# A new written order for five engines, new release points for late loads, and wider declarations of independence, in a fused attention and gated-convolution kernel

## The chip, the cores and the metric

The kernel runs on one core of one Trainium2 chip. The metric is device time in microseconds (us) for one execution; smaller is better. The engines are called PE (matrix products), ACT (activations and copies), DVE (vector arithmetic), POOL (here mostly the issue of software DMAs) and SP (the issue of hardware DMAs and DMA transposes).

## What is computed

There are 4 batches, 8 heads, 768 positions and 64 features per head. The attention is block sparse: 24 blocks of 32 positions, of which a query block sees its neighbours, the first and the last block, and three sampled ones. Its result, 512 features per position, goes through a feed-forward part with a depthwise convolution as the gate.

```python
scores = scale * np.matmul(q, k.transpose(0, 1, 3, 2))
scores = np.where(mask, scores, -1000000000.0)
attn = np.exp(scores - np.max(scores, axis=-1, keepdims=True))
attn = attn / (np.sum(attn, axis=-1, keepdims=True) + 1e-09)
x = np.matmul(attn, v)                       # then heads side by side: 512 features
h = np.maximum(x @ w_in, 0.0)                # 1024 features
conv_out = sum(conv_w[j] * hp[:, j:j + S, :] for j in range(3))   # hp is h, padded by one position
out = (h * (1.0 / (1.0 + np.exp(-conv_out)))) @ w_out
```

## The kernel before

**Units and segments.** The masked scores are taken densely: the mask is 24 more rows of the score product. The work is cut into 144 units. A unit is one PSUM tile of 128 keys by 1024 query columns (`st`, two of them): two halves of score products (operation `s`, line 746), one exponential on ACT over all 1024 columns (`exp`, line 757), which writes one of eight buffers `pt`, and two halves of four times two products with V (`av`, line 779). Units are numbered in the order in which they are worked; 18 of them make a segment, half a batch, and the last half batch is cut into a segment of 12 units and one of 6, so that there are nine segments, n = 0 to 8.

**A segment after its units.** DVE takes reciprocals and normalises (`rcp`, `norm`), the token tile is transposed by a DMA on SP (`x_xb`), or for seven tiles by PE with a copy behind it (`x_tr`, `x_cp`). Then come, for each of 8 groups of 128 features, the first product (`f1`, line 895, into one of two PSUM tiles `mix`), a relu out of PSUM into the feature tile `hE` on ACT (line 915) or on DVE (line 917), and, for each pair of groups, the convolution on DVE (`mul` line 949, `add` line 959), a tanh on ACT (`tanh`, line 998) and the gate on DVE (`g1` line 1001, `g2` line 1006). The segment n = 8 has its convolution on PE (`conv`, line 970). The second product (`f2`, line 825, line 810 for the last block of 128 rows) goes into `mix` too, is copied out by ACT or DVE (`ev`, through the helper `dcopy` at lines 328 and 330) and stored by a DMA on SP (`out`). While the feed-forward part of one segment is worked, the units of the next go on.

**Loads.** K, Q and V of a pair of heads are loaded by POOL. The pairs P = 0 to 3 belong to batch 0, and so on. From batch 2 on, each of these loads stands behind a `pace`: a copy of one element of the buffer `pt` of a named unit, by which POOL waits until the exponential of that unit is done. Such a copy reads `pt`, so the exponential that writes the same buffer eight or more units later has to wait for it.

**What sets the order.** Every operation is entered in a list `gr.ops` with its engines and an assumed cost for each, a due time, dependences and buffers. A search outside the kernel found an order; its result stands in the string `ORDER`. Only this string decides what is issued: for each operation it names the engine, where there is a choice, and the buffer. `put_down` walks through it, and calls the function that issues the instructions.

```python
            o = ops[64 * CODE.index(line[x]) + CODE.index(line[x + 1])]
            engines = list(o.alts)
            e = engines[0]
            if len(engines) > 1:
                e = ENGINES[line[x]]
            for b in o.allocs:
                b.index = CODE.index(line[x])
            if o.fn is not None:
                o.fn(e)
```

Costs, due times, earliest times and dependences in the list are not looked at here. The framework below adds a semaphore wait wherever two instructions on different engines touch the same tile and one of them writes. It takes a tile's columns in strides coarsely, which is why `apart` declares some pairs of instructions on `hE` independent: those that touch other columns of it.

## Time and profile before

| | |
|---|---|
| time of three executions, median (lowest to highest) | 204.87 us (204.59 to 204.95) |
| span of the profiled execution, first to last instruction | 202.8 us |
| time of the profiled execution itself | not listed apart from its span; the median lies 2.07 us above the span |
| busy PE, ACT, DVE, POOL | 196.8, 189.7, 181.8, 57.5 us |
| granted TensorE clock, mean | 0.998 |

A busy time is the union of an engine's instructions, in which pipelined matmuls overlap. A group of instructions shows its busy time, the mean duration of one in nanoseconds (with the overlap counted in), and the idle time of its engine ahead of it with what ended it. The chain of waits is followed back from the last instruction: it names, for each stretch of time, the instruction that held up the end.

### The profile page before, as it was taken

What the parts mean: (1) busy time and instruction counts of PE and PEld (TensorE: products, weight loads), DVE (VectorE), ACT (ScalarE), POOL (GpSimd) and SP (SyncE); (2) the same over time, 40 slices, a digit from 0 to 9 for tenths busy, and PEclk for the clock granted to TensorE, in tenths of its full rate; (3) what the DMA queues carried; (4) which work ended last, traced back from release to release, by engine and by line L of the source; (5) the groups of instructions that cost most, each with busy time, mean ns of one, the idle gap of its engine ahead of it and who ended that gap; (6) DMA issues with size and microseconds to landing.
All of it is one profiled execution on the core that took longest, in us unless ns stands there. A gap on an engine that the chain in (4) does not pass through costs nothing.

```text
span 202.8 us, 6814 instructions
## 1 busy us (share of the span) xinstructions
PE 196.8 (97%) x2708; PEld 153.9 (76%) x2708; DVE 181.8 (90%) x572; ACT 189.7 (94%) x251; POOL 57.5 (28%) x112
## 2 busy tenths in 40 slices
PE   7899999999999999999999999999999999999993
PEld 7799977986788777877688877876678877876742
DVE  7999989999999979999899988999899968999950
ACT  6999999999999999999999998999999989998842
POOL 8870568630520354202534328400000000000000
PEclk9999999999999999999999999999999999999999
DMA  6999999999998399956869699994321202001515
GB/s 143 177 223 207 182 135 132 167 171 151 155 122 129 61 141 154 213 106 132 133 108 159 82 197 218 135 176 115 124 72 24 41 14 68 13 10 60 204 63 202
DMA packets 53655, 25.96 MB, mean 128 GB/s; under 512 B 39616, under 2 KB 50584, under 8 KB 53624
## 3 DMA queue, kind: packets, MB, share of 16 engines
q0 software_dynamic: 19984, 11.24, 43.7%
q1 hardware_dynamic: 33208, 13.87, 34.6%
q8 instruction: 21, 0.34, 0.7%
q10 hardware_dynamic: 432, 0.43, 0.6%
q14 instruction: 10, 0.08, 0.1%
HBM read 23.08 MB, written 6.29 MB: 145 GB/s over the span
## 4 chain that ended last, share of the span: by engine, by line
PE 78%; ACT 15%; issue 3%; DVE 2%; DMA 1%; ACTq 0%
PE st L746 25%; PE mix L895 18%; PE mix L825 17%; PE av L779 14%; ACT pt L757 11%; DMA o2s<-in_k_dram 1%; DVE e L330 1%; ACT m L998 1%; PE mix L810 1%; PE st L825 1%; PE av L970 1%; ACT nat L328 1%; PE mix L508 1%; ACT hE L915 0%; ACT o2s L328 0%
## 5 line engine op out<-in xcount | busy, mean ns | idle before, releaser
L757 ACT ACTIVATE pt<-st 128x1024 bf16<-128x1024 f32 x144 | 140.6, 1039 | 1.8 <-PE st L746 0.9
L779 PE MATMUL av<-vt,pt 128*128 128x65 bf16 x1152 | 59.9, 193 | 0.2 <-DVE vt L330 0.2
L779 PEld LDWEIGHTS <-pt 128*128 128x128 bf16 x1152 | 52.3, 97 | 9.9 <-issue 0.3
L895 PE MATMUL mix<-xT,winb 128*128 128x384 bf16 (+2 forms) x288 | 53.6, 308 | 0.1
L949 DVE TENSOR_SCALAR m<-hE,cw 128x382 bf16<-128x382 bf16 (+2 forms) x192 | 49.3, 316 | 0.5 <-ACT hE L915 0.2
L825 PE MATMUL mix<-woutb,gT 128*128 128x512 bf16 x176 | 47.1, 379 | 0.3 <-DVE gT L1006 0.3
L746 PE MATMUL st<-o 88*128 88x128 bf16 (+1 forms) x240 | 43.9, 229 | 0.4 <-ACT pt L757 0.3
L746 PE MATMUL st<-o,e 88*128 88x128 bf16 (+1 forms) x228 | 43.4, 233 | 0.0
L746 PE MATMUL st<-e,o 88*128 88x128 bf16 (+1 forms) x224 | 42.3, 234 | 0.2 <-ACT pt L757 0.2
L746 PE MATMUL st<-e 88*128 88x128 bf16 (+1 forms) x208 | 40.9, 239 | 0.1
L746 PEld LDWEIGHTS <-o 88*128 88x128 bf16 x464 | 34.7, 97 | 7.7 <-issue 0.8
L746 PEld LDWEIGHTS <-e 88*128 88x128 bf16 x436 | 33.0, 97 | 7.1 <-issue 0.4
L959 DVE TENSOR_TENSOR m<-m 128x764 bf16<-128x764 bf16 (+2 forms) x64 | 33.5, 532 | 0.4
L895 PEld LDWEIGHTS <-winb 128*128 128x128 bf16 x288 | 24.0, 97 | 8.0 <-issue 0.5
L998 ACT ACTIVATE m<-m 128x764 bf16<-128x764 bf16 (+2 forms) x32 | 26.3, 829 | 0.5 <-DVE m L959 0.3
L825 PEld LDWEIGHTS <-gT 128*128 128x128 bf16 x184 | 15.0, 97 | 9.3 <-DVE gT L1006 0.5
L417 POOL COPY pace<-pt 1x1 bf16<-1x1 bf16 x24 | 6.2, 257 | 49.9 <-ACT pt L757 49.8
L1006 DVE TENSOR_TENSOR gT<-m,hE 128x764 bf16<-128x764 bf16 (+3 forms) x36 | 18.0, 510 | 0.5
L698 DVE TENSOR_TENSOR xtok<-av,rcp 128x384 bf16<-128x384 f32 (+2 forms) x36 | 18.2, 506 | 0.3
L915 ACT ACTIVATE hE<-mix 128x384 bf16<-128x384 f32 (+2 forms) x36 | 17.7, 507 | 0.7 <-PE mix L895 0.5
L240 POOL DMA_DIRECT2D nat<-in_q_dram x23 | 16.8, 733 | 3.2 <-issue 2.5
L917 DVE TENSOR_SCALAR hE<-mix 128x384 bf16<-128x384 f32 x28 | 15.3, 549 | 2.6 <-PE mix L895 2.2
(84 smaller groups left out, 157.4 us busy)
## 6 DMA issues: line engine op xcount, KB each, us to landing
out_dram<-o2s SPq DMA_DIRECT2D x23, 256.0 KB
vn<-in_v_dram POOLq DMA_DIRECT2D x16, 192.0 KB, 5.0
nat<-in_k_dram POOLq DMA_DIRECT2D x15, 192.0 KB, 4.7
nat<-in_q_dram POOLq DMA_DIRECT2D x7, 192.0 KB, 5.2
winb<-in_moe_w_in_dram POOLq DMA_DIRECT2D x2, 512.0 KB, 9.5
woutb<-in_moe_w_out_dram POOLq DMA_DIRECT2D x4, 256.0 KB, 8.2
nat<-in_q_dram POOLq DMA_DIRECT2D x8, 96.0 KB, 4.5
nq<-in_q_dram POOLq DMA_DIRECT2D x5, 96.0 KB, 5.2
```

What stands on the lines that cost most here:

```text
L240: return op(name, {eng: occ}, lambda e: on(e).dma_start(out=dst(), in_=src), prio, deps, dma=(kind, service), **kw)
L698: nm = op("norm", {"DVE": t_dps(128 * C)}, lambda e: nc.vector.tensor_tensor(out=xtok_t[xk.index][:, 0:C].rearrange("p c h d -> p h c d"), ...
L746: nc.tensor.matmul(out=st[:, 128 * x:128 * (x + n_)], lhsT=QK[kc % 2][s][0:88, 1, hh, kc // 2, :], rhs=QK[par][s][0:88, 0, hh, idx:idx + n ...
L757: nc.scalar.activation(out=pt_t[ptb.index], in_=st_t[stb.index], func=AF.Exp, bias=0.0, scale=0.125)
L779: nc.tensor.matmul(out=o[:, off:off + 65], lhsT=pt_t[ptb.index][:, 128 * x:128 * x + 128], rhs=V_t[vslot_b[P].index][:, hh, kc, 0:65], sta ...
L825: nc.tensor.matmul(out=acc(), lhsT=gT_t[gb.index][:, ffc, 128 * t:128 * t + 128], rhs=woutb[:, ffc, :], start=(ffc == 0), stop=(ffc == NFF ...
L895: nc.tensor.matmul(out=mix_t[hb.index][:, w1 * y:w1 * y + w1], lhsT=winb[:, fc, 128 * ffc:128 * ffc + 128], rhs=xT_t[xt_buf[n].index][:, f ...
L915: i = nc.scalar.activation(out=dst, in_=src, func=AF.Relu, bias=0.0, scale=0.5)
L949: i = nc.vector.tensor_scalar(out=m_t[cb.index][:, x, y, 0:w], in0=hE_t[heb.index][:, f0 + y, t0 + x:t0 + x + w], scalar1=cw[:, x, f0 + y: ...
L959: nc.vector.tensor_tensor(out=m[:, a_, :, 0:w], in0=m[:, a_, :, 0:w], in1=m[:, b_, :, 0:w], op=ALU.add)
L998: th = [op("tanh", {"ACT": t_act(2 * w) + 0.04}, lambda e, cb=cb, w=w: nc.scalar.activation(out=m_t[cb.index][:, 0, :, 0:w], in_=m_t[cb.in ...
L1006: i = nc.vector.tensor_tensor(out=gT_t[gtb.index][:, f0:f0 + 2, t0:t1], in0=m_t[cb.index][:, 0, :, 0:w], in1=hE_t[heb.index][:, f0:f0 + 2, ...
```

## The change

It leaves every computation as it is, and does four things.

1. `ORDER` is replaced. The list of 1789 operations is the same, and each stands in the new string once; the sequence on every engine is another, 44 operations change their engine, and buffers are dealt out anew.
2. The units on which the 24 paced loads of batches 2 and 3 wait are a list now, one number for K, Q and V of each pair.
3. `apart` is called for every segment. It declares a relu independent of the convolution instructions of earlier segments of the same batch, and of the relus of earlier segments of that batch on the other engine, where before only the segments n = 6 and 7 had this, between them.
4. The assumed costs, earliest times and dependences in the operation list are changed in some forty places. The load of the sampled blocks is entered through another helper, with the same DMA on the same queue.

The core of the diff, with the strings left out:

```diff
-    def PACE_U(P):
-        b, j = divmod(P, 4)
-        return 36 * (b - 1) + ((12, 17, 22, 28) if b == 1 else (4, 12, 20, 27))[j]
+    PACES = (27, 22, 32, 32, 27, 59, 39, 55, 50, 35, 40, 66, 0, 45, 71, 33, 74, 80, 42, 60, 99, 12, 88, 108)
...
-        pc = pace(PACE_U(P), due - 14) if b > 1 else None
+        pc = pace(PACES[3 * (P - 8)], due - 14) if b > 1 else None
...
-            pq = pace(PACE_U(P) + 2, due - 12)
+            pq = pace(PACES[3 * (P - 8) + 1], due - 12)
...
-                pv = pace(PACE_U(P) + 4, due - 9)
+                pv = pace(PACES[3 * (P - 8) + 2], due - 9)
...
-        e_op = op("exp", {"ACT": t_act(1024)}, e_fn, T(u), s_ops, alloc=[ptb], uses=[stb])
+        e_op = op("exp", {"ACT": t_act(1024) + 0.006}, e_fn, T(u), s_ops, alloc=[ptb], uses=[stb])
...
-    def apart(n, pr, x, inst):
-        if n in (NSEG - 3, NSEG - 2):
-            for other in side.get((pr, 1 - x), []):
+    def apart(n, pr, x, inst, e):
+
+        for other, by in side.get((n, pr, 1 - x), []):
+            if by != e:
                 tc.declare_no_dep(inst.ins, other.ins, reason="other columns of the feature tile")
-            side.setdefault((pr, x), []).append(inst)
+        side.setdefault((n, pr, x), []).append((inst, e))
+
+    wrote = {}
...
-                if n == NSEG - 2:
-                    apart(n, fg, 0, i)
+                for m in range(n):
+                    if SEGS[m][0] == SEGS[n][0]:
+                        for y in range(FB * fg // 2, (FB * fg + FB - 1) // 2 + 1):
+                            apart(m, y, 0, i, e)
+                for y in range(FB):
+                    for other, by in wrote.get((SEGS[n][0], FB * fg + y), []):
+                        if by != e:
+                            tc.declare_no_dep(i.ins, other.ins, reason="other columns of the feature tile")
+                    wrote.setdefault((SEGS[n][0], FB * fg + y), []).append((i, e))
...
-                        if n == NSEG - 3:
-                            apart(n, f0 // 2, 1, i)
+                        apart(n, f0 // 2, 1, i, e)
...
-                if n == NSEG - 3:
-                    apart(n, f0 // 2, 1, i)
+                apart(n, f0 // 2, 1, i, e)
```

Read out of the two strings, the operations that change their engine are these (fg is the group of features):

| operation | from ACT to DVE | from DVE to ACT |
|---|---|---|
| relu | n=0: fg 3, 6, 7; n=1: 3, 4, 6; n=2: 3, 5, 6; n=4: 2, 7 | n=0: fg 2; n=2: 2, 7; n=4: 1, 6; n=5: 3; n=6: 5 |
| ev | 9, of which one is half a tile wide | 3 |
| v_cp (V into its padded tile) | 2 | |
| start: casts, mask and K/Q copies of pair 0 | 6 | 4 |
| x_cp | | 1 |

One store (`out`, rows 512 to 639 of the last batch) goes from SP's queue to ACT's. The mix of score halves and feed-forward products on PE has the same instructions in another sequence.

166 lines of the change are left out of this document (82 added, 84 removed).

## The prediction

> **What bounds the kernel now.** I read the page's head and its chain of waits first, then the busy times by stretches, then the chain by pieces.
>
> ```profile
> span 202.8 us, 6814 instructions
> ...
> PE 196.8 (97%) x2708; PEld 153.9 (76%) x2708; DVE 181.8 (90%) x572; ACT 189.7 (94%) x251; POOL 57.5 (28%) x112
> ...
> PE 78%; ACT 15%; issue 3%; DVE 2%; DMA 1%; ACTq 0%
> ```
>
> Three engines are over 90% busy, so work can't be moved off one without landing on a full one. The shares of the chain are averages; the stretches tell more. I cut them where the first exponential starts (7.58), where exponential 54 does (65.89; rows of both stand below), and where DVE runs out of work (195.40).
>
> ```profile
> 7.58:65.89 58.31, 57.49 (x908) 48.60 (x906) 54.86 (x166) 57.81 (x69) 25.53 (x50) 1.00 1.20 163
> 65.89:195.40 129.51, 129.09 (x1713) 97.47 (x1711) 120.95 (x375) 123.80 (x166) 25.51 (x48) 1.00 0.63 110
> ```
>
> The columns are start:end, length, then busy PE, weight load, DVE, ACT, POOL. In the first stretch ACT is busy all but 0.50 us, DVE all but 3.45. In the second ACT has 5.7 idle, DVE 8.56. The chain of waits between 36 and 70 us says who decides there:
>
> ```profile
> by line: ACT pt L757 60.1%; issue 16.5%; PE st L746 6.9%; ACT m L998 6.0%; PE mix L825 3.8%; ACT hE L915 2.9%; PE av L779 2.5%; PE mix L470 1.0%; PE mix L895 0.5%; ACTq L757 0.1%; ACTq L915 0.1%
> ```
>
> ACT decides up to 67 us; from there the chain runs through PE, pieces end to end. How much PE can give back is bounded by its own work, priced with pieces of the chain (start, length, line, count) and counts of the page:
>
> ```profile
> 6.54 0.59 PE st L746 x6
> ...
> 19.59 0.45 PE mix L508 x8
> ...
> 24.91 0.44 PE st L746 x6
> ...
> 28.22 0.65 PE mix L895 x4
> ...
> 65.89 1.06 ACT pt L757
> ...
> 73.66 0.86 PE mix L825 x4
> ...
> 90.54 0.73 PE av L779 x24
> ...
> 178.88 0.87 PE mix L895 x8
> ...
> 189.12 0.59 ACT o2s L328
> ...
> 191.50 0.45 PE mix L895 x8
> ...
> 197.81 1.76 PE mix L810 x16
> ```
> ```profile
> L757 ACT ACTIVATE pt<-st 128x1024 bf16<-128x1024 f32 x144 | 140.6, 1039 | 1.8 <-PE st L746 0.9
> L779 PE MATMUL av<-vt,pt 128*128 128x65 bf16 x1152 | 59.9, 193 | 0.2 <-DVE vt L330 0.2
> ...
> L895 PE MATMUL mix<-xT,winb 128*128 128x384 bf16 (+2 forms) x288 | 53.6, 308 | 0.1
> ...
> L825 PE MATMUL mix<-woutb,gT 128*128 128x512 bf16 x176 | 47.1, 379 | 0.3 <-DVE gT L1006 0.3
> ```
>
> Scores: 144 units x 0.44 = 63.4. Products with V: 1152 x 0.73/24 = 35.0. First product, 224 wide ones x 0.65/4 = 36.4, and by the code 32 of 256 columns x 0.87/8 = 3.5 and 32 of 128 x 0.45/8 = 1.8. Second product: 176 and, by the code, 8 more in the tail, x 0.86/4 = 39.6, and 1.8 at the end. Some 115 transposes, fillers and convolution products x 0.45/8 = 6.5. Sum 188.0. From the first score at 6.54 to the last product's end at 199.57 are 193.0, so PE has 5.0 us of spare. In the first 18 units nothing else is there for it: ACT gives a unit in 0.93 (row below, 4.66/5), PE needs 0.44 + 8 x 0.030 = 0.68 for it, 18 x 0.25 = 4.5, less some 45 transposes and fillers, 2.5: 2.0 can't be had. About 3.0 us is the ceiling for any order, beside an earlier start.
>
> [...]
>
> **The change part by part.** *Costs, earliest times, dependences in the list:* nothing; `put_down` reads none of them. *Declarations:* in the strings I counted the convolution instructions that stand behind a relu of a later segment on the same features on another engine: none in batches 0 to 2, in either string; four pairs before and six after in the last batch. So the declarations release no instruction in the first three batches. For the last I take 0, at most 0.3, half of the piece at 189.12, where the chain leaves PE for ACT; a loss is excluded, as a wait is only dropped.
>
> *Engine moves.* Busy time over count of each form is the price:
>
> ```profile
> L917 DVE TENSOR_SCALAR hE<-mix 128x384 bf16<-128x384 f32 x28 | 15.3, 549 | 2.6 <-PE mix L895 2.2
> L915 ACT ACTIVATE hE<-mix 128x384 bf16<-128x384 f32 x28 | 13.7, 510 | 0.1
> ...
> L328 ACT COPY o2s<-mix 128x512 f32<-128x512 f32 x14 | 8.2, 591 | 2.8 <-PE mix L825 2.7
> ...
> L330 DVE COPY o2s<-mix 128x512 f32<-128x512 f32 x8 | 5.5, 690 | 4.1 <-PE mix L825 4.1
> ...
> L330 DVE COPY vt<-vn 128x768 bf16<-128x768 bf16 x14 | 5.3, 388 | 0.1
> ...
> L330 DVE COPY xT<-mix 128x384 bf16<-128x384 bf16 x4 | 1.4, 355 | 0.5 <-PE mix L717 0.4
> ...
> L328 ACT COPY vt<-vn 128x768 bf16<-128x768 bf16 x2 | 1.7, 872 | 0.0
> ```
>
> Net over the kernel, four relus, six evictions (one of half size) and two V copies leave ACT, one `x_cp` comes: 4 x 0.49 + 5.5 x 0.59 + 2 x 0.85 - 0.35 = 6.6 us less on ACT. On DVE 4 x 0.55 + 5.5 x 0.69 + 2 x 0.38 - 0.35 = 6.4 us more. The start is priced apart.
>
> *Ahead of exponential 54*, ACT's new queue has 3 relus instead of 8, 6 gate tanhs as before, one eviction and one `x_cp` more: -5 x 0.49 + 0.59 + 0.35 = -1.5 us. That is on the path. DVE in turn gets, up to about exponential 60, five relus, and loses an eviction and an `x_cp`: 5 x 0.55 - 0.69 - 0.35 = +1.7.
>
> *The start.* Rows of the timeline (start, length, engine):
>
> ```profile
> 0.74 2.87 DMA o2s<-in_k_dram
> ```
> ```profile
> 1.18 0.46 ACTq L240 DMA_DIRECT2D o2s<-in_k_dram  x1
> ...
> 2.97 0.61 ACT L298 ACTIVATE o<-nblk 24x128 bf16<-24x128 bf16 x2
> ...
> 3.64 0.77 ACT L328 CAST nat<-o2s 128x384 bf16<-128x384 f32 x2
> ...
> 4.61 0.85 DVE L314 TENSOR_SCALAR e<-may 24x144 bf16<-24x144 bf16 x4
> ...
> 4.96 0.47 ACT L328 COPY e<-mix 64x384 bf16<-64x384 bf16 x1
> ...
> 5.45 0.26 ACT L328 COPY o<-mix 64x128 bf16<-64x128 bf16 x1
> ...
> 5.74 0.35 ACT L328 CAST nat<-o2s 128x192 bf16<-128x192 f32 x1
> 6.12 0.37 ACT L328 COPY e<-mix 64x256 bf16<-64x256 bf16 x1
> ...
> 7.58 4.66 ACT L757 ACTIVATE pt<-st 128x1024 bf16<-128x1024 f32 x5
> ```
>
> Before, ACT does mask rows, two casts, a mask copy, the K copy, a Q copy, the third cast, a Q copy, a mask copy and two Q copies. The new queue is: mask rows, cast of K of head 0 (0.77 less the 0.35 of a Q cast, some 0.45), cast of K of head 1 (the same; its DMA was issued about 0.44 behind the first, so it should have landed by 4.05), K copy, both Q copies of head 0, last Q cast, the second K copy of head 0, exponential 0, another K copy, exponential 1. That is 3.64 + 2 x 0.45 + 0.47 + 0.37 + 0.26 = 5.64 for what the first score waits on (its mask from DVE ends at 5.46), 0.9 before 6.54; then 0.35 + 0.47 = 6.46 for exponential 0, 1.1 early; the copy behind it takes 0.47 back, so 0.6 early from exponential 1 on. DVE must follow: behind the mask it has three mask copies, copies of K and Q, mask slots, a V copy and those of pair 1, and by the same kind of sum they end within about half a microsecond of where unit 4 asks for them. So 0 to 0.6; I take 0.4.
>
> *Release points.* POOL's paced loads are off the path:
>
> ```profile
> POOL pace L417 <- ACT pt L757: 49.8, 15, 9.9
> ```
>
> POOL idles 49.8 us at its paces. The new points pull K of pairs 8 to 12 together around unit 41 to 47, where before they went out between 46 and 79; their use is at unit 72 and later, 25 units of 1.08 us off ((65.89 - 7.58)/54), some 27 us. The work that hides them is the units between. What is queued behind a late pace on POOL is later loads; who waits is ACT: in the new string the copy that reads unit 22's buffer stands behind exponential 42, one load issue deep in POOL's queue, and exponential 44 writes that buffer. At the worst the two units between are the price, 2.2 us at one such place; I take 0, since POOL was early at all 15 waits above.
>
> *Tail.* The last two evictions and the store that ACT now issues lie behind the same 16 products of 1.76 us; the store's eviction on DVE, 0.69, ends well before the last one. 0.
>
> *Sum.* First stretch: ACT would give 0.4 + 1.5 = 1.9. But DVE had 3.45 idle there and gets 1.7 more work, so the stretch can shrink by 1.75 only if DVE has not one gap left. Between 0.4 (the start alone) and 1.75 I take 1.2, nearer the upper end, because the chain there passed through ACT and not through DVE. Second stretch: ACT's relief is off the path, PE's work is the same: 0. Span 202.8 - 1.2 = 201.6. The median stands 2.07 above the span, which I keep: 203.7 us.
>
> **The rivals.** *More: DVE doesn't bind.* The new string also puts off DVE work past exponential 54: two normalisations, two convolution multiplies (of two instructions each), two adds and a gate fewer stand ahead of it. Then ACT's 1.9 comes whole, and some of PE's remaining spare of 3.0: 1.9 to 3.0 less, 201.9 to 203.0, middle 202.4. For it: the stretch's chain. Against: what is put off has to be done in the next stretch.
>
> *Nothing:* pair 1's copies on DVE hold up unit 4 and eat the start, and the five relus on DVE hold `mix`, so that PE gets the first product's tiles no earlier: 204.9.
>
> *Slower: DVE's in-order queue becomes the bound of the second stretch.* It has 8.56 idle and gets 6.4 - 1.7 = 4.7 more work, leaving 3.9. An eviction blocks its queue until the second product is done: 4.1 us were lost at 5 of 8 evictions, 0.82 each. Six more at 0.65 use up the 3.9; with the 1.2 gained before, the kernel is slower than now from 0.85 each on. At 1.1, between the 0.82 and the longest wait of 1.7, six make 6.6: 6.6 - 3.9 - 1.2 = 1.5 later, 206.4. For it: the same `mix` pair serves first and second product, so a late eviction stops PE too. Against: an order can put an eviction where its product is done.
>
> [...]
>
> **How the numbers follow.** A measurement of this kernel tells apart about 0.2%, 0.41 us. The forecast, 203.7 (203.1 to 204.5), has a chance of 0.48; more, 0.16; nothing, 0.08; slower, 0.28. Faster by over 0.2% (below 204.46): 0.46 + 0.16 = 0.62. Within: 0.02 + 0.06 = 0.08. Slower: 0.28 and 0.02 of the rest, 0.30. The range runs from 202.1, which leaves 0.04 below, to 206.4, which leaves half of the slow case, 0.14, above. The forecast's own range stands above, as cases of both signs hold much of the chance.
>
> **What would show it.** Right: exponential 0 near 6.5 and exponential 54 near 64.7; ACT near 183 busy and DVE near 188; in the stretch up to exponential 54 a DVE with under 1 us idle; PE's work end to end behind it. The start is wrong if exponential 9 comes as late as before. The slow rival shows as DVE waiting for evictions by over 8 us in all, with PE waiting for DVE behind them. A pace that holds ACT would show as an exponential waiting for POOL. The prediction is wrong if the time is under 203.0 with DVE full, or above 204.5.

## The result: slower by 3.3%

The kernel after takes 212.31 us (median of four executions, 210.51 to 214.46) against 204.73 (204.38 to 204.95) in the same comparison: a ratio of 1.0334, with a 95% interval of 1.0260 to 1.0408. The forecast was 203.7 us with 206.4 as the upper end of its range. The profiled execution took 211.26 us, 1.8 over its span. Its executions spread over 4 us where those of before spread over half a microsecond here, and over up to 4.6 us in the comparisons further down (204.21 to 208.85); the half clock shown below, which differs from execution to execution, is one reason (the mean clock of after's four is 0.992 in the one of 210.51 us and 0.976 in the one of 214.46). Every profile is of one execution, and those of e1, e9 and e15 below are of slow ones (216.75, 230.92 and 216.93 us), so their stretches are on the long side.

The page of the kernel after: head, busy times, granted clock by slices, and shares of the chain of waits.

```profile
span 209.5 us, 6813 instructions
...
PE 199.4 (95%) x2708; PEld 155.6 (74%) x2708; DVE 185.2 (88%) x585; ACT 185.1 (88%) x238; POOL 60.3 (29%) x112
...
PEclk9969999999969999999999999999999999999999
...
PE 81%; DVE 13%; DMA 2%; ACT 1%; issue 1%; ACTq 0%; DVEq 0%
```

ACT fell from 189.7 to 185.1 and DVE rose from 181.8 to 185.2: 4.6 less and 3.4 more, where the sum over the moves, without the start, had said 6.6 and 6.4. ACT has left the chain (15% before, 1% now), but DVE stands in it with 13%, and a DMA with 2%. Two slices have a granted clock of 0.6.

To find the place, I cut both profiles at exponentials 12, 42 and 54 (before: 18.77, 51.67, 65.89; after: 20.65, 53.57, 72.16, counted off in ACT's timeline). Columns: start:end, length, busy PE, weight load, DVE, ACT, POOL, granted clock, DMA share, GB/s. First the kernel before:

```profile
7.58:18.77 11.19, 10.73 (x192) 9.85 (x190) 10.31 (x29) 11.03 (x13) 5.93 (x9) 1.00 1.32 209
18.77:51.67 32.90, 32.54 (x510) 27.10 (x507) 30.80 (x97) 32.62 (x40) 15.75 (x34) 1.00 1.29 160
51.67:65.89 14.22, 14.22 (x213) 11.65 (x211) 13.75 (x42) 14.17 (x19) 3.85 (x8) 1.00 0.91 131
65.89:202.80 136.91, 133.24 (x1739) 99.92 (x1736) 120.96 (x375) 126.20 (x171) 25.51 (x48) 1.00 0.62 112
```

The same cuts in the kernel after:

```profile
6.42:20.65 14.23, 12.86 (x190) 11.55 (x187) 10.88 (x26) 12.21 (x14) 6.84 (x11) 0.88 1.30 197
20.65:53.57 32.92, 32.36 (x519) 27.05 (x517) 30.81 (x104) 32.33 (x38) 17.89 (x36) 1.00 1.06 146
53.57:72.16 18.59, 15.16 (x207) 11.98 (x206) 13.69 (x40) 13.74 (x18) 8.30 (x18) 0.91 1.06 143
72.16:209.50 137.34, 133.84 (x1747) 100.36 (x1744) 125.02 (x388) 122.40 (x163) 21.63 (x36) 1.00 0.61 108
```

The span grew by 6.7 us: 1.9 up to exponential 12 (20.65 - 18.77), nothing from 12 to 42, 4.4 from 42 to 54 (18.59 - 14.22), 0.4 from there to the end. The gain of the forecast, a shorter way to exponential 54, did not come, and the two large losses are both in stretches where an engine waits for copies or DMAs. Both of these stretches of after also hold 3.41 us at half clock.

**The start.** Chain of waits of after:

```profile
8.44 0.50 DVE vt L328
8.96 0.88 DVE e L328
9.87 0.88 DVE e L328 x2
10.79 0.30 DVE o L328
```

From 8.4 to 11.1 DVE's queue decides: the V copy of pair 0, a mask copy, the copies of pair 1, and only then may PE take the scores of unit 4. PE is idle for part of it, and directly behind this the clock is halved. Stretches of after:

```profile
8.00:11.20 3.20, 1.94 (x27) 1.39 (x25) 3.08 (x7) 2.82 (x3) 2.33 (x5) 0.99 1.27 174
11.20:14.60 3.40, 3.40 (x43) 3.15 (x43) 2.68 (x6) 2.05 (x2) 2.04 (x3) 0.50 1.36 216
```

**Exponentials 42 to 45.** Chain of waits of after:

```profile
51.41 0.27 DVE xtok L694
...
54.09 5.07 DMA xT<-xtok
59.16 0.04 issue
59.20 1.12 PE mix L894 x3
```

```profile
DVE e L328 <- DMA stg<-nat: 3.8, 1, 3.8
PE mix L894 <- DMA xT<-xtok: 3.4, 1, 3.4
```

The second fence is from the waits: us in all, times, longest. PE stands for 3.4 us in front of the first product of segment 1, because the last of the four transposes of that segment's result (`x_xb`, tile `xT`) lands at 59.16; before, it landed at 53.00. In the same time DVE stands in front of K and Q of pair 7, which SP brings by transposes too (`xb`, into the staging tile `stg`, from where DVE copies them, `stg_cp`). Behind PE's stop the clock is again halved:

```profile
55.50:59.00 3.50, 0.27 (x2) 0.04 (x1) 0.94 (x3) 1.42 (x2) 3.50 (x8) 0.99 1.25 171
59.00:62.40 3.40, 3.20 (x19) 2.14 (x19) 2.51 (x6) 1.02 (x1) 2.75 (x5) 0.51 1.39 194
```

How the transpose came to be late can be followed in both traces. Its normalisation began on DVE at 51.32 instead of 46.21 (the chain counts it from 51.41, when the instruction ahead of it is over). DVE's timeline, before and then after:

```profile
46.21 0.55 DVE L698 TENSOR_TENSOR xtok<-av,rcp 128x384 bf16<-128x384 f32 x1
```
```profile
51.32 0.55 DVE L694 TENSOR_TENSOR xtok<-av,rcp 128x384 bf16<-128x384 f32 x1
```

Of these 5.1 us, 3.3 were there when the first of the four was normalised (37.89 instead of 34.56), 1.9 of them from the start; the rest is DVE's fuller queue between the two. Stretch from the first to the last of these normalisations, before and then after:

```profile
34.56:46.21 11.65, 11.64 (x205) 10.08 (x203) 11.54 (x37) 11.65 (x16) 5.57 (x11) 1.00 1.43 158
```
```profile
37.89:51.32 13.43, 12.88 (x224) 10.84 (x223) 13.26 (x39) 12.96 (x16) 4.11 (x6) 1.00 1.15 155
```

DVE has 13.26 us of work there instead of 11.54 and no gap to speak of in either. Counted from exponential 42, the normalisation begins 5.45 us ahead in before and 2.25 us ahead in after. In all of e1 to e16 below, whose DVE and PE have the order of after but for a few operations, it is 2.2 to 2.4 us, also in e14, where seven relus are back on their old engines. So it is the written order, and not those relus, that took 3.2 us of cover from this transpose.

The rest of the way is SP's. The normalisation ends at 51.87, and SP was free at 52.19. But there stands a transpose of pair 7 in after's order, and the issue of it took SP 1.81 us. SP's timeline of after (start, length of the issue):

```profile
52.19 1.81 SPq L581 DMA_TRANSPOSE stg<-nat  x1
```

So the transpose went out at 54.09, 1.9 us after it could have, and took 5.07 us to land. In the traces of before and of after, 51 transposes each, all land in the order in which SP issued them, and the one of pair 7 ahead of it landed at 57.93. In e10 below, where it is issued ahead of pair 7's, it lands after 2.28 us. In before the way from the end of this normalisation to the landing was 6.2 us, in after it is 7.3: set against before, most of the lateness is the normalisation's, and SP's order kept it from being made up.

### The profile page after: what moved, and what is told of

The parts are those of the page before. It is cut to its first block, busy times and chain, and to the rows that moved or that the text cites. A ratio compares the mean times of both kernels' runs of the same rounds, so it can differ in the third digit from the quotient of the medians.

```text
span 209.5 us, 6813 instructions
## 1 busy us (share of the span) xinstructions
PE 199.4 (95%) x2708; PEld 155.6 (74%) x2708; DVE 185.2 (88%) x585; ACT 185.1 (88%) x238; POOL 60.3 (29%) x112
## 4 chain that ended last, share of the span: by engine, by line
PE 81%; DVE 13%; DMA 2%; ACT 1%; issue 1%; ACTq 0%; DVEq 0%
PE st L742 26%; PE mix L894 18%; PE mix L821 17%; PE av L775 14%; DVE m L955 3%; DMA xT<-xtok 2%; PE st L1031 2%; DVE e L328 2%; DVE o L328 1%; DVE m L964 1%; DVE hE L916 1%; DVE gT L1011 1%; PE mix L806 1%; PE st L821 1%; DVE xtok L694 1%
## 5 line engine op out<-in xcount | busy, mean ns | idle before, releaser
L775 PEld LDWEIGHTS <-pt 128*128 128x128 bf16 x1152 | 50.6, 98 | 10.0 <-issue 1.1
L894 PE MATMUL mix<-xT,winb 128*128 128x384 bf16 (+2 forms) x288 | 54.2, 311 | 3.6 <-DMA xT<-xtok 3.4
L775 PE MATMUL av<-vt,pt 128*128 128x65 bf16 x1152 | 56.8, 194 | 0.7 <-DVE vt L328 0.7
L955 DVE TENSOR_SCALAR m<-hE,cw 128x382 bf16<-128x382 bf16 (+2 forms) x192 | 48.2, 310 | 1.8 <-ACT hE L914 1.6
L821 PE MATMUL mix<-woutb,gT 128*128 128x512 bf16 x176 | 47.7, 379 | 0.0
L742 PE MATMUL st<-e,o 88*128 88x128 bf16 (+1 forms) x224 | 43.1, 237 | 0.1
L742 PE MATMUL st<-e 88*128 88x128 bf16 (+1 forms) x208 | 42.2, 244 | 1.0 <-ACT pt L753 0.6
L742 PEld LDWEIGHTS <-e 88*128 88x128 bf16 x436 | 33.5, 98 | 10.0 <-issue 1.8
L894 PEld LDWEIGHTS <-winb 128*128 128x128 bf16 x288 | 23.9, 98 | 11.5 <-issue 4.3
L916 DVE TENSOR_SCALAR hE<-mix 128x384 bf16<-128x384 f32 x32 | 17.5, 550 | 3.3 <-PE mix L894 2.9
L914 ACT ACTIVATE hE<-mix 128x384 bf16<-128x384 f32 (+2 forms) x32 | 15.7, 499 | 1.1 <-PE mix L894 1.1
```

Source lines behind the costliest of these rows:

```text
L742: nc.tensor.matmul(out=st[:, 128 * x:128 * (x + n_)], lhsT=QK[kc % 2][s][0:88, 1, hh, kc // 2, :], rhs=QK[par][s][0:88, 0, hh, idx:idx + n ...
L775: nc.tensor.matmul(out=o[:, off:off + 65], lhsT=pt_t[ptb.index][:, 128 * x:128 * x + 128], rhs=V_t[vslot_b[P].index][:, hh, kc, 0:65], sta ...
L821: nc.tensor.matmul(out=acc(), lhsT=gT_t[gb.index][:, ffc, 128 * t:128 * t + 128], rhs=woutb[:, ffc, :], start=(ffc == 0), stop=(ffc == NFF ...
L894: nc.tensor.matmul(out=mix_t[hb.index][:, w1 * y:w1 * y + w1], lhsT=winb[:, fc, 128 * ffc:128 * ffc + 128], rhs=xT_t[xt_buf[n].index][:, f ...
L916: i = nc.vector.tensor_scalar(out=dst, in0=src, scalar1=0.5, scalar2=0.0, op0=ALU.mult, op1=ALU.max)
L955: i = nc.vector.tensor_scalar(out=m_t[cb.index][:, x, y, 0:w], in0=hE_t[heb.index][:, f0 + y, t0 + x:t0 + x + w], scalar1=cw[:, x, f0 + y: ...
```

## The experiments

The names of the theories in the expectations. Q: queues that are in order stand behind a DMA that is late. B: the run of ten loads on POOL at 53 to 61 us (release points of K of pairs 8 to 12 and others) slows the transposes. D: Q and B together. V: DVE has no room, and its late normalisations are the cause. In the diffs the operations of one queue stand in their order; "x_xb 0" to "x_xb 3" are the four transposes of segment 1, "xb P5" a transpose of pair 5. The runs below are told by this table, worked out from exponentials 12, 42 and 54 and the span of each profile:

| kernel | time, us | to exp. 12 | 12 to 42 | 42 to 54 | 54 to end | half clock, us |
|---|---|---|---|---|---|---|
| before | 204.7 to 205.3 | 18.77 | 32.9 | 14.2 | 136.9 | 0 |
| after | 212.31 | 20.65 | 32.9 | 18.6 | 137.3 | 6.8 |
| e1 | 214.46 | 19.80 | 33.4 | 24.5 | 137.3 | 10.2 |
| e3 | 221.82 | 19.70 | 33.2 | 29.7 | 137.3 | 13.7 |
| e4 | 213.92 | 19.27 | 35.7 | 20.0 | 137.3 | 6.8 |
| e5 | 211.56 | 19.66 | 32.9 | 19.1 | 138.0 | 3.4 |
| e6 | 220.69 | 19.26 | 33.7 | 25.2 | 142.1 | 13.7 |
| e7 | 235.74 | 19.64 | 34.4 | 19.6 | 158.7 | 23.9 |
| e8 | 224.32 | 19.89 | 32.9 | 22.1 | 147.6 | 10.2 |
| e9 | 226.24 | 19.21 | 33.1 | 23.7 | 153.2 | 23.9 |
| e10 | 210.55 | 20.57 | 33.0 | 18.7 | 137.3 | 6.8 |
| e11 | 210.73 | 19.35 | 32.7 | 19.4 | 137.3 | 6.8 |
| e12 | 208.27 | 19.46 | 33.2 | 16.6 | 137.3 | 0 |
| e13 | 210.75 | 19.01 | 33.2 | 19.3 | 137.3 | 6.8 |
| e14 | 211.55 | 19.46 | 33.1 | 19.7 | 137.5 | 3.4 |
| e15 | 217.25 | 19.45 | 32.9 | 20.5 | 142.3 | 10.2 |
| e16 | 209.81 | 19.66 | 32.9 | 18.3 | 137.3 | 3.4 |
| b1 | 210.85 | 18.93 | 36.8 | 14.5 | 138.9 | 3.4 |
| b2 | 204.87 | 18.61 | 33.4 | 14.9 | 136.9 | 0 |
| b3 | 205.22 | 18.43 | 32.9 | 14.2 | 138.2 | 0 |

The last column leaves out the clock's fall at the end of the program (from 201.99 us in before, from 209.13 in after). The times are medians, for before over several comparisons; the stretches are of one execution each. b2, which takes as long as before, has 1.3 us more from exponential 12 to 54 in its profile, so a difference of that size between two rows says little.

### The parts of the change, alone, in the order of before

**b2**, the declarations alone: the source of after with the string and the release points of before.

```diff
-                if n == NSEG - 2:
-                    apart(n, fg, 0, i)
+                for m in range(n):
+                    if SEGS[m][0] == SEGS[n][0]:
...
```

> The order and release points of the kernel before, with the declarations of the kernel after alone. The prediction's term is 0, at most 0.3 less: 204.5 to 205.2. A gain or loss of over 0.4 us would show that the declarations release something.

Ratio 0.9978 (0.9955 to 1.0001): the declarations release nothing that can be measured.

**b3**, the release points alone.

```diff
 POOL, behind the loads of pair 7:
-  nq P4, K P8, Q P8, K P9 (unit 48), V P8, Q P9, V P9, K P10 (56), ... K P11 (63), ... K P12 (76)
+  nq P4, K P8, Q P8, K P9 (43), K P10 (44), V P8, Q P9, K P11 (46), K P12 (47), ... V P9, ...
```

> The kernel before with the release points alone changed, as far as its order allows: K of pairs 9 to 12, Q of pair 9 and V of pair 8 let go by exponentials 42 to 47 in one run behind Q of pair 8, as in after; all else (PE, ACT, DVE, SP's order) as before. The prediction's term for release points was 0: 204.5 to 205.2. Theory B (a burst of loads beside transposes costs): transposes issued between 49 and 60 us land 2 to 4 us later, DVE waits for a staging tile, 206 to 209.

Ratio 0.9996 (0.9959 to 1.0034). The lateness that theory B names is there, its cost is not: the transpose of pair 8 issued at 55.21 landed after 11.7 us instead of some 3.1, the other one at 58.69 after 15.4 instead of 5.8, but nobody needed them sooner. DMA share of the same five microseconds, before and then b3:

```profile
60.00:65.00 5.00, 5.00 (x88) 4.30 (x86) 4.94 (x18) 5.00 (x7) 1.28 (x3) 1.00 1.08 132
```
```profile
60.00:65.00 5.00, 5.00 (x88) 4.26 (x86) 4.94 (x18) 5.00 (x6) 0.89 (x2) 1.00 1.74 77
```

PE, DVE and ACT do the same work in that time in both. In this order, the price of 0 was right.

**b1**, seven relus alone.

```diff
-  relu n=0: fg 3, 6, 7 on ACT, fg 2 on DVE;  n=1: fg 3, 4, 6 on ACT
+  relu n=0: fg 3, 6, 7 on DVE, fg 2 on ACT;  n=1: fg 3, 4, 6 on DVE
```

> The kernel before, with only the engines of seven relus ahead of exponential 54 as in the kernel after: six from ACT to DVE, one from DVE to ACT, each at its old place in the order. The prediction's term (ACT decides, DVE can take 1.75): exponential 54 1 to 2 us earlier, 203.0 to 204.0. Rival V (DVE has no room, its queue is in order): exponential 54 no earlier or later, 205 to 207.

Ratio 1.0276 (1.0253 to 1.0299): 5.6 us slower, of which the 3.41 us of half clock from 45.12 on cost up to 1.7. Rival V, more strongly than it had said. Chain of waits of b1 around the last moved relu of segment 0, and the wait in DVE's timeline:

```profile
37.80 0.67 PE mix L895 x4
...
38.56 0.56 DVE hE L917
...
44.76 0.48 DVE xtok L698
45.23 0.04 issue
45.28 0.38 PE av L779 x4
```
```profile
38.56 0.56 DVE L917 TENSOR_SCALAR hE<-mix 128x384 bf16<-128x384 f32 x1 [2.57 <-PE mix L895]
```

The relu came to its turn on DVE 2.6 us ahead of the product that it reads. All behind it waited with it: convolutions, K and Q copies, and the normalisation that frees the PSUM tile of the next V products. The busy sum on which the forecast rested (ACT less 2.45, DVE more 2.75) has no place for that.

**e14**, the other way round: the kernel after, with those seven relus on their old engines, each at its place in the order of after.

```diff
-  relu n=0: fg 3, 6, 7 on DVE, fg 2 on ACT;  n=1: fg 3, 4, 6 on DVE
+  relu n=0: fg 3, 6, 7 on ACT, fg 2 on DVE;  n=1: fg 3, 4, 6 on ACT
```

> The kernel after, with the seven relus ahead of exponential 54 on the engines of before (six back on ACT, one back on DVE), each at its place in the order of after. If the moves of after paid in its own order, this is slower than after: 213 to 215. If a fuller DVE is what makes the last normalisation of segment 1 late, exponential 45 comes earlier than 61.3 and it is faster: 209 to 211.

211.55 us, ratio 1.0328 (1.0261 to 1.0395) to before, no different from after's 1.0334. In the order of after the moves neither pay nor cost: exponentials 12 to 42 take 33.1 and 32.9 us, and the wait for `xT` is 3.6 and 3.4. Neither of the two expected times came.

### The start of after

**e4**, the start order of before on PE and DVE in the kernel after.

```diff
 PE:
-  ... av unit 0, s unit 3 ...
+  ... s unit 3, av unit 0 ...    (4 fillers ahead of each of two scores)
 DVE:
-  V copy of pair 0, mask copy, K and Q copies of pair 1
+  mask copy, K and Q copies of pair 1, V copy of pair 0
```

> Only the first 12 us of PE's and DVE's queues differ from the changed kernel: the V copy of pair 0 stands behind the copies of pair 1 on DVE, the first two products with V behind the scores of unit 4 on PE, and eight fillers ahead of units 3 and 4, as in the kernel before. Theory S (the start is lost because the V copy and its product with V stand ahead of what unit 4 needs, and PE then idles long enough that its clock is halved from 11.2 to 14.6 us): exponential 4 near 11.0 instead of 11.5, no slow stretch there, exponential 6 near 13 instead of 14.8: 1.5 to 2 us less, 210.5. Rival (mask slots and copies of pair 1 on DVE set it whatever stands beside them): exponential 4 and 6 within 0.3 us of now, 212.

**e5**, 24 more fillers on PE (products of a constant tile that nobody reads) between 8 and 13 us.

```diff
-    NFILL = 12
+    NFILL = 36
```

> The changed kernel with 24 more filler matmuls of 128 columns (56 ns each, their result unused) on PE between 8 and 13 us, where PE waits; every other queue as changed. Theory C (the clock is halved because PE idled about 1.9 us of the 3.4 us before): the stretch at half clock around 11 to 14.6 us is gone, 1.5 us less, 210.8, with exponential 4 still at 11.5. If the clock is lowered by something else, the slow stretch stays, and the time is 212.3 plus up to 0.5.

e4 takes 213.92 us, ratio 1.0410 (1.0352 to 1.0467), more than either of its expectations had said. Both keep the full clock in the start: 1.00 from 11.20 to 14.60. The 1.9 us of theory C are what PE was busy in after from 8.00 to 11.20 (1.94); it idled for 1.26. But so do e1 and e12, whose queues up to there are those of after, while e10's profile has the half clock at the same place as after's. So with the order of after the halving comes in some executions and not in others (the last section sets the starts side by side), and that it stayed away in e4 and e5 proves nothing for these two edits. Without it exponential 12 stands at 19.26 (e6) to 19.89 (e8), with it at 20.6: the order costs 0.5 to 1.1, the half clock 0.7 to 1.4 more. The four kernels with the start order of before on PE and DVE (e4, e9, e11, e13) stand at 19.01 to 19.35, still 0.2 to 0.6 behind before, so only part of the loss is that order's. What e4 gained it lost later, with 35.7 us from 12 to 42, as PE then waited for the two mask copies that stand behind x_xb 0 on SP (0.8 to 2.4 us each). e5 is at 211.56, ratio 1.0304 (1.0234 to 1.0374), not to be told from after.

### Queues that stand behind a DMA

**e1**, SP's queue:

```diff
-  xb P7, x_xb 2, xb P7, x_xb 3
+  x_xb 2, x_xb 3, xb P7, xb P7
```

> Only SP's queue differs from the changed kernel: the two transposes of pair 7 (stg) are put behind the token transpose of segment 1, heads 6 and 7 (x_xb), as they stood in the kernel before. Theory Q (the stall of the first product at 55.4 us comes from that token transpose standing in SP's queue behind transposes that wait for the late Q load of pair 7): the 3.4 us wait of PE for xT is gone, and with it the second stretch of 3.4 us at half TensorE clock (1.7 us): 212.3 - 5.2 = about 207. Theory B (the burst of K loads that starts at 54.2 us slows whatever transpose is under way): the token transpose goes out some 3 us earlier, partly ahead of the burst, 208 to 211. Theory D (DVE is the bound around 30 to 54 us anyway, so the next wait of PE follows at once): 211 or more.

No better than after: 214.46 us, ratio 1.0437 (1.0382 to 1.0493). PE's wait for `xT` at exponential 45 went, exponential 45 stands at 57.77 instead of 61.27, and the stop came one step later. Waits of e1, from 40 to 84 us:

```profile
DVE e L329 <- DMA stg<-nat: 8.0, 3, 6.4
ACT hE L915 <- PE mix L895: 6.8, 1, 6.8
PE mix L895 <- DVE hE L917: 6.5, 1, 6.5
```

DVE's copies of pair 7 stand ahead of segment 1's first relus in after's order; the copies waited for their transpose, the relus for the copies, PE for the relus.

**e10**, the same with these two copies moved behind the first relus and multiplies of segment 1.

```diff
 DVE (besides e1's edit of SP):
-  stg_cp P7, rcp, stg_cp P7, v_cp, norm, relu fg 1, v_cp, relu fg 0, 3 mul, add, relu fg 3, add, 2 mul
+  rcp, v_cp, norm, relu fg 1, v_cp, relu fg 0, 3 mul, add, relu fg 3, add, 2 mul, stg_cp P7, stg_cp P7
```

> The kernel after, with the transpose of segment 1's last normalisation ahead of pair 7's on SP (as in e1) and, besides, DVE's two copies out of pair 7's staging tile moved behind the first relus and multiplies of segment 1, so that a late transpose of pair 7 holds up no relu. Theory Q (the stall is made by in-order queues that stand behind a DMA: PE behind xT, DVE behind the staging tile): exponential 45 near 57.8, DVE's wait for the staging tile under 2 us instead of 8.0, exponential 54 near 69 instead of 72.2, 208 to 210. Rival B (the load burst makes every transpose late, so any order of them leaves a stall): exponential 54 at 72 or later, 212 or more.

210.55 us, ratio 1.0228 (1.0146 to 1.0310). Exponential 48 stands at 59.93, 5.1 us ahead of after, and then PE has to wait for pair 7 itself, whose transpose takes 8 us; exponential 54 stands at 72.35, as late as B had it. Chain of waits of e10:

```profile
54.55 8.00 DMA stg<-nat
...
63.03 0.55 DVE e L329
...
64.22 0.27 PE st L743 x2
```

**e12**, the same with the loads spread.

```diff
 POOL (units that release them, besides e10's edits):
-  K P7, Q P7 (33), V P7 (39, 32), K P8 (27), K P9, K P10, Q P8, V P8, nq P4, Q P9, K P11, K P12
+  K P7, Q P7, V P7, nq P4 (40), K P8, Q P8 (42), V P8 (44), K P9 (47), K P10 (48), Q P9 (48), K P11 (49), K P12 (50)
```

> As e10, with POOL's loads spread: V of pair 7 behind its Q at once, then the second Q of pair 4, K, Q and V of pair 8 as the release points of before let them go, and K and Q of pairs 9 to 12 released by exponentials 47 to 51 instead of in one run at 53 to 61 us. Theory B (the burst of ten loads is what makes the transposes of pair 7 take 5 to 8 us): that transpose lands within 5 us of its issue, PE's wait for pair 7's copies (3.7 + 3.2 in e10) goes, exponential 54 near 68, 205.5 to 208. Rival (the order of after leaves pair 7 too little time in any case): exponential 54 at 71 or later, 209 to 211.

208.27 us (208.05 to 210.82), ratio 1.0210 (1.0128 to 1.0293), which can't be told from e10's ratio. Its profile has no half clock outside the end. From exponential 42 to 54 it takes 16.6 us instead of e10's 18.7 and before's 14.2; the other 1.1 us to e10 are the start. But pair 7's transpose still took 7.5 us (53.58 to 61.04), and waits for pair 7's copies are left:

```profile
PEld L743 <- DVE e L329: 2.6, 1, 2.6
PE st L743 <- DVE e L329: 2.4, 1, 2.4
```

In e10 the first of these was 3.2. So the wait itself shrank by little; most of the 2.1 us is the half clock that follows it in e10's profile (0.50 from 65.70 to 69.00) and not in e12's. The executions say the same: the one of e10 with a mean clock of 1.0 took 208.35 us, the three of e12 with a mean clock of 1.0 took 208.05 to 208.36. Spreading the loads has no gain of its own here that the runs show; whether it makes the half clock rarer (three of four executions in e10, one of four in e12) is too little to tell. So these runs show no price of theory B in this order either, as in that of before (b3).

**e3**, the burst put off whole, with all else as after.

```diff
 POOL:
-  V P7, K P8, K P9, K P10, Q P8, V P8, nq P4, Q P9, K P11, K P12
+  V P7, (exponential 50), K P8, K P9, K P10, Q P8, V P8, nq P4, Q P9, K P11, K P12
```

> Only POOL's queue differs from the changed kernel: the run of nine loads with its paces, from K of pair 8 to K of pair 12, stands behind exponential 50 instead of exponentials 41 to 48. SP's queue is as changed. Theory Q: the token transpose is still issued at 54.1, behind the Q transpose of pair 7; without loads beside it it lands some 2 us earlier (57 instead of 59.2), PE's wait is 1.5 instead of 3.4 us, the slow clock may stay: 210 to 211. Theory B: its landing comes within 2 us of the issue and PE hardly waits: 207 to 208. If neither, no change, 212.

The edit held back too much: among the nine was the second Q of pair 4, which was needed at once. 221.82 us, ratio 1.0806 (1.0763 to 1.0848), with 9.3 us of `PE mix L505 <- DMA nq<-in_q_dram`. What it shows for the question is that the transpose took 4.21 us instead of 5.07, with PE's wait for it 2.5: without the burst beside it, it was still slow, and landed 0.9 us behind pair 7's.

**e11** and **e13**, e10 and e12 with the start order of before and the two mask copies first on SP; **e16**, e12 with the mask copies and pair 5's transposes ahead of x_xb 0.

```diff
 SP:
-  x_xb 0, mask, mask, xb P5, xb P5, x_xb 1, ...
+  mask, mask, x_xb 0, xb P5, xb P5, x_xb 1, ...    (e11, e13)
+  mask, mask, xb P5, xb P5, x_xb 0, ...            (e16, e15)
```

> As e10, with the start order of PE and DVE of the kernel before, and the two mask copies on SP ahead of the first transpose. Theory Q: exponential 12 at 19.3, exponential 36 below 46, no PE wait for the masks, exponential 54 near 67, 206 to 208. Rival B: the lead is lost between exponentials 42 and 54, 211 or more.

> As e12, with the start order of before on PE and DVE and the two mask copies on SP ahead of the first transpose. Theory B: 1.4 us under e12, 204 to 206.5; this is the repaired kernel, and what it is worth against before is then the true value of the moves from ACT to DVE. Rival: 208 to 210.

> e12 with the same early issue on SP (mask copies and pair 5's transposes first). Theory Q: pair 7's transpose lands by 57 instead of 61.0, the 5.0 us that PE and its loads wait for pair 7's copies fall under 1.5, exponential 54 near 67.5, 205.5 to 207. Rival: no better than e12's 208.3.

210.73, 210.75 and 209.81 us, ratios 1.0277 (1.0240 to 1.0314), 1.0295 (1.0268 to 1.0323) and 1.0215 (1.0161 to 1.0268). e13 and e16 were to be better than e12 and are not. The earlier copies did not bring pair 7 forward: in e16 pair 7's transpose went out at 53.82 and landed at 61.33, as late as in e12. These expectations, on theory Q and for e13 on theory B, failed; the profiles of all three hold half clock again (6.8, 6.8 and 3.4 us).

**e15**, the DMA queues of after alone: the masks and pair 5's transposes first on SP, loads spread, DVE as after.

> The kernel after with three edits of its DMA queues alone (PE, ACT and DVE in the order of after): SP issues the two mask copies and pair 5's two transposes ahead of the transpose of segment 1's first normalisation, so that these no longer stand behind it; the rest of SP's order as after; POOL's loads spread as in e12. Theory Q (in-order SP queue: its head waited for a late normalisation, and all that stood behind came 3 to 5 us late): pair 7's transpose lands by 55 instead of 57.9, exponential 45 near 57, no wait of PE for xT over 1 us, exponential 54 near 68.5, 206.5 to 208.5. Rival V (the normalisation on DVE is late in itself): the wait for xT stays at 2 us or more, exponential 54 at 70 or later.

217.25 us (211.79 to 219.81), too spread for an interval. PE's wait for `xT` stayed, as rival V had it, but not for V's reason: the last normalisation was done on DVE by 50.66, and x_xb 3 went out at 54.25 (and landed at 59.47), because the transpose of pair 7 ahead of it held SP from 51.40 for 2.75 us. So the place in SP's queue, which this kernel had left as in after, is enough for the wait. That the normalisation itself is late (2.24 us ahead of exponential 42) is so here too.

### Queues of before with engines of after

**e6**: SP's DMAs in the order of before, output stores as after; **e7**: POOL's loads and release points of before; **e8**: both; **e9**: both, and e4's start.

```diff
 SP (e6, e8, e9):
-  x_xb 0, mask, mask, xb P5, xb P5, x_xb 1, xb P6, xb P6, xb P7, x_xb 2, xb P7, x_xb 3
+  mask, mask, x_xb 0, xb P5, xb P5, xb P6, xb P6, x_xb 1, x_xb 2, x_xb 3, xb P7, xb P7
 release points (e7, e8, e9):
-    PACES = (27, 22, 32, 32, 27, 59, 39, 55, 50, 35, 40, 66, ...
+    PACES = (40, 42, 44, 48, 50, 52, 56, 58, 60, 63, 65, 67, ...
```

> The kernel after, with the DMAs of SP's queue (mask copies and transposes) in the order of before; output stores, loads, PE, ACT and DVE as after. Theory D (the 4.7 us lost between exponentials 42 and 45 come from the DMA queues): with the mask copies out early and the transposes of the norms ahead of those of pair 7, exponential 45 stands near 57.5 instead of 61.3, the PE wait for xT goes, and the time is 208 to 210 if the load burst then delays other transposes, near 207 if not. Rival V (DVE is full and its late normalisations are the cause): exponential 45 stays at 60 or later, 211 to 213.

> The kernel after, with POOL's loads in the order and with the release points of before; all other queues as after. Theory D: no burst of loads at 53 to 61 us; transposes land in under 5 us; the mask copies and the transposes of pair 7 still stand ahead of that of the last normalisation, so a wait of 1 to 2 us at exponential 45 is left: 208 to 210. If the release points cost nothing, as predicted: 212, exponential 45 near 61. Rival V: 211 to 213.

> Both of these together: POOL's loads with their release points and SP's queue as before; PE, ACT and DVE in the order of after. Theory D: what is left is the loss of the start, 1.9 us at exponential 12, so exponential 54 near 67.5 and 206.5 (205.5 to 208). Rival V: exponential 45 later than 58.5 and 209 to 213.

> As the one with both queues of before, and the start order of PE and DVE as before too (first V copy behind the copies of pair 1, first product with V behind the scores of unit 3, four fillers ahead of each of two scores). Theory D with the start loss apart: exponential 12 at 19.3, no half clock in the start, exponential 54 near 66.0, 205.0 (203.5 to 206.5); the moves of work from ACT to DVE alone would then be worth about nothing. Rival V: exponential 12 early, the lead gone by unit 45, 208 to 212.

220.69, 235.74, 224.32 and 226.24 us, ratios 1.0760 (1.0662 to 1.0858), 1.1523 (1.1425 to 1.1621), 1.0919 (1.0850 to 1.0988) and 1.0871 (1.0778 to 1.0963). All four expectations failed, by 11 to 26 us over the upper end that theory D gave. e8 has one half of theory D: exponential 45 stands at 56.37, and from 42 to 45 it takes 3.6 us, where after takes 7.7 and before 3.0. So other DMA queues take away 4.1 of the 4.7 us that after loses between these two; e10's edit on SP and DVE takes away 4.5. Then DVE's queue, in which pair 7's copies stand where after's SP would have served them, waits 6 us for the transpose that before's SP serves later. Chain of waits of e8:

```profile
54.16 5.87 DMA stg<-nat
60.12 0.55 DVE e L329
...
62.74 1.44 PE mix L895 x4
```

e7 loses 22 us of its 31 behind exponential 54, where DVE waits 16.3 us for staging tiles in four places and 17.1 us are at half clock. The likely reason, not tested, is that after's copies ask for their pairs sooner than before's release points give them.

## Why the prediction was wrong

**The step that failed** is the first stretch of the sum, "Between 0.4 (the start alone) and 1.75 I take 1.2": busy sums of ACT and DVE, set against their idle time, with 0 for the release points. The stretch up to exponential 54 did not shrink by 1.2 us but grew by 6.3 (72.16 for 65.89).

**What the sum lacked.** I put 0 by the 27 us between the new loads and their own use. b3 shows that price to be right in the order of before, e10 and e12 show none in that of after, and no exponential waited for POOL. But the change also reordered SP, and no step went through SP's queue, in which both mask copies were moved behind x_xb 0 and a transpose of pair 7 ahead of x_xb 3. Nor did any step ask how long ahead of its use the last normalisation of segment 1 now stands (3.2 us less), nor where in DVE's queue stand the copies that wait for pair 7. The first stop, at exponential 45, is shown to hang on SP's and DVE's queues: with x_xb 3 ahead of pair 7's transpose and the two copies behind the first relus (e10 to e13, e16), exponentials 42 to 45 take 3.2 us, where after takes 7.7 and before 3.0. But the time was not won back, as the next stop, at pair 7, came behind it, and what each place is worth alone can't be read off.

**The clock** has no term in the sum either. The two stretches of half clock in after's profile cost up to 1.7 us each, so up to 3.4 of the 6.7 us; both follow on gaps of PE (busy for 2.15 and for 0.23 of the 3.41 us ahead of them).

**The start** was to bring 0.4 us and lost 0.5 to 1.1, and 1.9 in the profile with the half clock. ACT's part of the step was right: exponential 0 came at 6.42, the sum had said 6.46. What failed there is "within about half a microsecond of where unit 4 asks for them": DVE's copies end at 11.1, and exponential 4 comes at 11.54 instead of 11.21. The sign named for it, exponential 9 as late as before, came: 17.65 against 16.06.

**ACT's relief ahead of exponential 54**, 1.5 us with DVE as the limit, was worth nothing. Half of the answer is in the table of windows: up to exponential 42 only three relus have left ACT, and one and an `x_cp` have come; ACT is 0.3 us less busy (32.33 for 32.62) and the stretch is as long as before; three of the relus come behind, where PE stood still. The other half are b1 and e14. The forecast took busy sums and a limit from idle time; a relu on DVE costs what DVE waits for the product, 2.6 us in one place in b1.

**Second stretch and tail** were set at 0 and lost 0.4 (137.34 for 136.91). The ceiling on PE's spare was not put to the test: no kernel run here takes under 136.9 from exponential 54 to the end.

**Declarations**: 0, as forecast (b2).

**The rivals.** The slower one had the right sign by the wrong mechanism. It named evictions that block DVE's queue; their waits fell from 4.1 us to 2.3. Its place was the second stretch, which lost 0.4. Waits of the kernel after:

```profile
DVE o2s L328 <- PE mix L821: 1.2, 2, 0.7
...
DVE o2s L328 <- PE st L821: 1.1, 1, 1.1
```

That an engine's order decides was right in kind, but what blocked was a copy on DVE and a product on PE that wait for a DMA, not evictions that wait for PE. Its upper end of 206.4 had no room for a loss from SP.

**What stays open.** No version here beats the kernel before; b2 and b3, which are it in all but the declarations or the release points, equal it. Some 2.4 us of e12's stretch from 42 to 54 remain, with the second transpose of pair 7 at 7.5 us, and 0.7 us of its start. In before that transpose took 4.4 us. It went out there with no load in flight (50.53; the next load at 51.45), in e12 with two (53.58; loads from 52.37 and 53.08). Whether that is the reason was not tested.

## What to carry to other kernels

Where several engines run in order, don't price a move by busy sums: go through every queue, those of the DMA issuers too, find the instruction ahead of the moved one and behind it, and ask what each waits for. A transpose's cover must be counted with the transposes that its queue issues ahead of it, not only for itself. An order written by a search is one piece: queues of one order with engines of another cost more here (7.6 to 15%) than one order differs from the other (3.3%), so test a part of it by a move within one queue, and expect the stop to move on.

## What the runs showed of the hardware

**The granted clock was halved for 3.41 us at a time.** In after's trace it is at half from 11.16 to 14.57 and from 58.95 to 62.36, and the two starts lie 47.79 us apart, 14 times 3.41. The totals in the last column of the table of the experiments, 3.4 to 23.9 us, are multiples of 3.41 too. Cut into pieces of this length from such a start on and back, and in before back from the clock's fall at 201.99, the traces of after and before have 57 pieces each at full clock from 7 us on. Four of these 114 have half clock behind them: the two of after shown here, 63% and 7% busy on PE, and the last whole piece of each program (0.48 us busy from 205.72 on in after, 0.98 from 198.58 on in before). Behind the other 110, with PE busy for 2.86 us or more, the clock was full. Stretches of after, each with half clock behind it:

```profile
7.75:11.16 3.41, 2.15 (x29) 1.58 (x27) 3.29 (x7) 3.04 (x4) 2.54 (x5) 1.00 1.26 173
55.54:58.95 3.41, 0.23 (x2) 0.01 (x1) 0.89 (x3) 1.38 (x2) 3.41 (x8) 1.00 1.23 171
```

In e12, with the same start order, the pieces lie elsewhere in the program, PE is idle for 0.38 us of one and 0.31 of the next, and the clock stays full:

```profile
6.62:10.03 3.41, 3.03 (x47) 2.75 (x45) 2.92 (x8) 3.08 (x5) 3.23 (x5) 1.00 1.33 191
10.03:13.45 3.42, 3.11 (x61) 2.73 (x59) 3.26 (x9) 3.40 (x5) 2.85 (x4) 1.00 1.34 220
```

From 8.00 to 11.20 us PE was busy for 1.94 us in after and 1.89 in e10, which run into half clock, and for 2.52 in e1 and 2.51 in e12, which do not. The matmuls of a stretch at half clock took about twice as long (six score products 0.85 us at 60.32 in after, 0.44 at 11.92 in before), so by my estimate each stretch costs up to 1.7 us, half its length. PE was not idle for the whole of a piece ahead of half clock: it was busy for 2.15 us in after's start, and for 1.69 in e10 (62.21 to 65.62). Why 63% was too little there, while e12 kept the full clock from 58.00 to 66.00 with PE busy for 5.20 of these 8.00 us, 65%, stays open, as does whether the place of a gap counts beside its length.

**The issue of a transpose had no fixed price.** The issue of one mostly took SP 1.2 us, but up to 2.4 us in after (74.52 and 167.53) and 2.9 in before (timeline of before):

```profile
41.11 2.93 SPq L585 DMA_TRANSPOSE stg<-nat  x1
```

What it waited for isn't seen in the trace: in before this issue and one at 46.36, which took 1.21 us, both had three transposes in flight.

**Transposes landed in the order of their issue, and later beside loads.** None of the 51 transposes of before and none of the 51 of after landed ahead of one that SP issued before it. Near the end of both programs, with no load of POOL in flight, a transpose landed 2.3 us after its issue (172.57 to 174.89 in before and 172.97 to 175.24 in after, DMA share 0.14 in both), and so did x_xb 3 in e10 with one load in flight (51.94 to 54.23). In the busy stretches of before and after it took mostly 3 to 10.5 us (the longest in before, 39.18 to 49.70, DMA share 1.45), and in b3 up to 15.4; the wait behind the transposes ahead is part of this. x_xb 3 of after, issued at 54.09, landed at 59.16 with the loads issued at 54.98 and 55.81 still in flight, up to 60.36 and 61.40.
